# A convolution and a gated feed-forward on one core: w_in's third block as one transfer, a one-head mask, the start's decode and first products in another order, twelve casts on GpSimd and some squares later

## The chip, the cores and the metric

The kernel runs on one core of a Trainium2 chip. Its engines are TensorE (PE, with its weight loads listed as PEld), VectorE (DVE), ScalarE (ACT), GpSimd (POOL) and SyncE (SP, which here issues all DMAs). Each engine works through its own queue in order; an instruction waits for the semaphores of others where it needs their results. The metric is the device time of one execution in microseconds (us). Three runs of the kernel before gave 1162.87, 1164.42 and 1164.15, a median of 1164.15.

## The reference

```python
def _attn_ref(x, weight):            # x: 8 x 4160 x 192, weight: 8 heads x 7
    w = np.exp(weight - np.max(weight, axis=-1, keepdims=True))
    w = w / (np.sum(w, axis=-1, keepdims=True) + 1e-09)
    # causal: position s gets its 6 predecessors and itself, zeros ahead of the start
    out = np.einsum('hk,bskhg->bshg', w, x_unf)      # a convolution per head of 24 channels
...
def _moe_ref(x, w_in, w_out, g_ln):  # x: 33280 x 192, w_in: 192 x 1024, w_out: 1024 x 192
    h = x @ w_in
    e = np.exp(h - np.max(h, axis=-1, keepdims=True))
    solu = h * e / (np.sum(e, axis=-1, keepdims=True) + 1e-09)
    mu = np.mean(solu, axis=-1, keepdims=True)
    var = np.mean((solu - mu) ** 2, axis=-1, keepdims=True)
    return ((solu - mu) / np.sqrt(var + 1e-06) * g_ln) @ w_out
```

`w_in` and `w_out` arrive as 64-bit floats. The kernel reads each as two 32-bit words and puts the value together itself.

## The kernel before, in words

**Tiles.** The 33280 rows are 260 tiles of 128. A tile goes through these helpers. `emit_rows` and `emit_third` (or, for the first two tiles, `emit_first`) multiply the convolved rows `yT` by w_in, kept as an upper and a lower half-precision part (`whi`, `wlo`), into two PSUM banks `ph` (L736, L749, L759). `emit_max` on DVE scales `ph` and takes the row's extreme (L790). `emit_exp` on ACT takes the exponential `e` (L797). `emit_mul` on DVE makes the product of `ph` and `e` (L807). `emit_hi` casts it to half precision (L815), `emit_lo` on GpSimd makes the rest of it (L827) and SP then issues a DMA that transposes both into `pT`. `emit_square` on ACT sums the squares (L819) for the variance. `emit_out` multiplies `pT` by w_out (`ohl`, L859) and `emit_evac` takes the result from PSUM to `raw` on DVE (L867, L869). After each group of up to eight tiles, GpSimd takes the roots (L927 to L931) and the rows are scaled and stored.

**Chunks.** The convolution works on chunks of x, ahead of the tiles. `load` brings pieces `xr`; `sum_squares` finds their size (`xj` on ACT, `xa` on DVE); `scale_steps` makes the scale `s` and the factors `cv` from it. From the fourth chunk (number 3) on each piece is split into `xs` halves (L234 to L243). `product` multiplies by the taps into one PSUM bank `pc` (L281), `upper` (ACT, L313) and `lower` (DVE, L322) write its two halves `y`, and DMAs transpose them into `yT`. `taps` come at the start from `band`, a mask times the softmaxed weights.

**The start.** Ahead of the first tile stands a sequence written out by hand: w_in's three blocks (columns 0 to 511, 512 to 1023 of the loaded rows, and the third, called `Z`, with the last 64 rows of w_in) go through the steps of class `Words`: `exponents`, `mantissas`, `join` (DVE; join puts the low word in), `powers` (ACT), `signs` (DVE), `value` (the product of join and signed powers), `squares` (ACT, for the size of w_in). From the size come five small DVE instructions that give `t_in`, the scale of w_in; only then `whi` and `wlo` can be written. w_out goes through the same kind of steps, with `lows` and `whole` on GpSimd in place of `join`, and with `out_powers`, which multiplies by `g_ln`.

**Order.** The program is recorded in the order of the code, under a manual schedule: an engine runs its instructions in just this order. `first_two`, `second_two`, `third_two` and `fourth_two` handle tiles 0 to 7 in pairs; `three_steps(i)` handles tiles i, i+1, i+2 from i = 8 on, with the convolution's work of the next chunk placed between; `last_three` ends it. In `three_steps`, `start` is true for i = 8, 11 and 14; `root_squares` emits squares left over from the triple before; `sum_up` sums squares of a chunk's piece. `queue.run` lets GpSimd's splitting steps in by a budget.

Of the kernel before, what the change touches and what calls it, by code (L numbers as in the profile page):

```python
# [19 lines left out]
def kernel(  # L20
# [366 lines left out]
    for j in range(2):  # L387
        nc.sync.dma_start(
            raw_in[j * R : (j + 1) * R, F:, :].rearrange("p f t -> p (f t)"),
            w_in[2 * R : D, j * F : (j + 1) * F],  # L390
        )
# [12 lines left out]
    pool.memset(band, 1.0)  # L404
    pool.affine_select(
        out=band, in_=band, pattern=[[0, H], [-1, TB], [-1, K]],
# [101 lines left out]
    def valued(c):  # L508

        wi.signs(c, wi.m)  # L510
        wi.value(c, wi.m, dve)
# [13 lines left out]
        band, band, wb.unsqueeze(2).broadcast_to([TJ, H, TB, K]), ALU.mult  # L525
# [12 lines left out]
    valued(halves[0])  # L538
# [48 lines left out]
    isq = cp.tile([P, 2], F32, name="isq")  # L587
# [19 lines left out]
    wi.squares(A, isq[:, 0:1])  # L607
    wi.signs(halves[1], wi.m)
    wi.exponents(Z)
    wi.powers(Z)  # L610
    for f in chain0[1:-3]:
        f()
    wi.squares(Z, isq[:, 1:2])
    for pc, hg in got0:
        c0.upper(pc, *hg)
    wi.value(halves[1], wi.m, dve)
    wi.mantissas(Z)
# [9 lines left out]
    for c in halves:  # L627
        act.activation(whi[:, 0, c], wi.f[:, c], AF.Copy, scale=t_in)
    settle(*spans0[0], got1)
# [3 lines left out]
    wo.lows(W, 2.0**-32)  # L633
    wi.join(Z)
    valued(Z)
    for pc, hg in got0:
        c0.upper(pc, *hg)
# [22 lines left out]
    wo.exponents(W)  # L660
    for f in chain0[-3:]:
        f()
    wo.mantissas(W)
    sums1 = [h for j in range(chunks[1].np) for h in chunks[1].halves(j)]
    wo.powers(W)
    wo.floats(W)
# [6 lines left out]
    gate = cp.tile([1, 1], F32, name="gate")  # L673
# [4 lines left out]
    mean = None  # L678

# [61 lines left out]
    def emit_first(t, u):  # L741
# [4 lines left out]
        for j, w, r in ((0, whi, 0), (2, whi, 0), (0, wlo, 0), (1, whi, 1)):  # L746
            for q, lhs in zip((t, u), y):
                for n, bank in enumerate(banks_of(q)):
                    nc.tensor.matmul(  # L749
                        bank, lhs[j], w[:, r, n * 512 : (n + 1) * 512],  # L750
                        start=j == 0 and w is whi, stop=False,
                    )
                for n in range(NH if r else 0):
                    emit_third(q, n, False, False)
# [57 lines left out]
    def emit_hi(t):  # L812
        t.halves = t.e.rearrange("p (n f) -> p n f", n=NH)
        t.p16 = sp.tile([P, NH, 2, 512], F16, name=f"p16_{t.i}", tag="p16", bufs=4)
        act.copy(t.p16[:, :, 0, :], t.halves)  # L815
# [333 lines left out]
    def first_two():  # L1149
# [4 lines left out]
        emit_exp(t)  # L1154
        wo.signs(W, wo.e)

        pool.tensor_copy(gate, wo.e.bitcast(F32)[0:1, 0:1])
        wo.whole(W)
# [16 lines left out]
    def second_two():  # L1175
# [13 lines left out]
        for f in scale:  # L1189
            f()  # L1190
# [104 lines left out]
    def three_steps(i):  # L1295
# [103 lines left out]
        if not start:  # L1399
            root_squares()  # L1400
# [197 lines left out]
```

## Time and profile before

| | before |
|---|---|
| runs, us | 1162.87, 1164.15, 1164.42 |
| span of the profiled execution, us | 1161.5 |
| the profiled execution's own time | one of these; the results don't say which, so 1.4 to 2.9 us lie around the span |
| PE idle, 0 to 44 us | 17.3 us |
| PE idle, 44 to 138 us | 5.9 us |
| PE idle, 138 us to the end | 5.6 us |

The idle times come from the busy times of stretches: 44 us less 7.87 and 18.88 us of work from 0 to 19 and from 19 to 44, for instance. A row of the timeline gives the start in us from the span's start, the duration, the engine, the line of the kernel, the operation, what it writes and reads, and in brackets how long its engine was idle before and what ended that. A row of the waits names who waited, for whom, the sum in us, how often and the longest. Groups of instructions end with busy us, mean ns of one and the idle time before them.

### The profile page before, as it was taken

The page shows a single profiled execution, that of the slowest core. Times are in us where ns is not written, and L with a number is a line of the kernel's source. Part 1 is how long each engine was busy: PE and PEld are TensorE (multiplying, and loading weights), DVE is VectorE, ACT ScalarE, POOL GpSimd, SP SyncE. Part 2 cuts the span into 40 slices and gives each one's busy share as a digit, 9 for nine tenths or more (in the row PEclk, how much of TensorE's full clock was granted, in tenths as well). Part 3 has the DMA queues.
Part 4 walks back from the last instruction along what each step waited for, and adds up shares of the span by engine and source line. Part 5 has one row for each costly group of instructions (what it writes and reads, how often), then busy time and mean ns, then how long its engine had stood idle before and what let it go on. Part 6 is the DMA issues. An engine that isn't in the chain of part 4 may idle for free.

```text
span 1161.5 us, 22374 instructions
## 1 busy us (share of the span) xinstructions
PE 1132.2 (97%) x7742; PEld 692.4 (60%) x7742; DVE 1016.8 (88%) x2058; ACT 998.0 (86%) x1775; POOL 878.6 (76%) x686
## 2 busy tenths in 40 slices
PE   5898999999999999999999999999999999999998
PEld 3575566656666665655656666665666566566556
DVE  8888898988989898998889989888898988788787
ACT  6998988888888888888888888898888889888886
POOL 2745879987888588887868888588788858855665
PEclk9999999999999999999999999999999999999999
DMA  8799899999999999999999999999999998999988
GB/s 226 171 181 180 185 218 205 205 201 202 200 213 195 195 186 220 207 189 199 202 198 190 208 209 199 187 202 208 206 204 198 195 193 170 174 177 186 181 163 188
DMA packets 727391, 226.95 MB, mean 195 GB/s; under 512 B 651614, under 2 KB 725870, under 8 KB 727278
## 3 DMA queue, kind: packets, MB, share of 16 engines
q1 hardware_dynamic: 727278, 225.53, 100.2%
q8 instruction: 60, 0.98, 0.3%
q14 instruction: 53, 0.43, 0.1%
HBM read 33.00 MB, written 25.56 MB: 50 GB/s over the span
## 4 chain that ended last, share of the span: by engine, by line
PE 88%; DVE 5%; ACT 2%; DMA 2%; issue 2%; POOL 1%; SPq 0%; DVEq 0%; ACTq 0%; POOLq 0%
PE po L859 40%; PE ph L736 36%; PE pc L281 6%; PE ph L759 5%; DVE e L807 1%; DMA pT<-p 1%; DVE ph L790 1%; DMA raw_in<-in_moe_w_in_dram 1%; ACT e L797 1%; ACT sq L819 0%; DVE raw L869 0%; DVE y L322 0%; POOL p L827 0%; PE mean L701 0%; DVE wlo L647 0%
## 5 line engine op out<-in xcount | busy, mean ns | idle before, releaser
L827 POOL TENSOR_TENSOR p<-e,p 128x1024 f16<-128x1024 f32 x257 | 548.3, 2138 | 219.5 <-ACT p L815 218.0
L859 PE MATMUL po<-ohl,pT 128*128 128x192 f16 (+1 forms) x4264 | 539.8, 283 | 7.8 <-DVE raw L869 5.4
L859 PEld LDWEIGHTS <-pT 128*128 128x128 f16 x4264 | 384.4, 98 | 167.1 <-issue 7.6
L736 PE MATMUL ph<-whi,yT 128*128 128x512 f16 x1548 | 419.1, 380 | 2.7 <-DVE e L807 2.6
L790 DVE TENSOR_SCALAR_CACHE_REDUCE ph<-ph,cv 128x1024 f32<-128x1024 f32 x248 | 319.1, 1288 | 72.9 <-PE ph L759 56.6
L797 ACT ACTIVATE e<-ph,sm 128x1024 f32<-128x1024 f32 x260 | 289.4, 1113 | 102.0 <-DVE ph L790 95.8
L807 DVE SCALAR_TENSOR_TENSOR e<-ph,cv,e 128x1024 f32<-128x1024 f32 x248 | 317.1, 1279 | 26.0 <-ACT e L797 25.7
L736 PEld LDWEIGHTS <-yT 128*128 128x128 f16 x2064 | 192.6, 98 | 231.3 <-issue 36.3
L815 ACT CAST p<-e 128x1024 f16<-128x1024 f32 x257 | 266.8, 1039 | 27.9 <-DVE e L807 27.3
L819 ACT ACTIVATE sq<-e 128x1024 f32<-128x1024 f32 x260 | 273.4, 1052 | 0.2
L736 PE MATMUL ph<-wlo,yT 128*128 128x512 f16 x516 | 153.5, 379 | 0.0
L869 DVE TENSOR_REDUCE raw<-po 128x192 f32<-128x384 f32 x247 | 136.3, 552 | 14.3 <-PE po L859 13.9
L243 POOL TENSOR_TENSOR xs<-xr,xs 128x960 f16<-128x960 f32 (+1 forms) x56 | 107.6, 1922 | 1.4
L313 ACT ACTIVATE y<-pc 112x432 f16<-112x432 f32 (+5 forms) x140 | 62.8, 469 | 13.8 <-PE pc L281 8.1
L759 PE MATMUL ph<-wlo,yT 64*128 64x512 f16 x269 | 74.0, 380 | 0.0
L322 DVE SCALAR_TENSOR_TENSOR y<-pc,y 112x432 f16<-112x432 f32 (+5 forms) x140 | 72.2, 532 | 0.8 <-ACT y L313 0.8
L281 PE MATMUL pc<-xs,taps_hi 128*112 128x240 f16 (+1 forms) x448 | 72.9, 261 | 0.0
L759 PE MATMUL ph<-wlo,y 64*128 64x512 f16 x251 | 68.6, 380 | 0.0
L181 DVE TENSOR_REDUCE xa<-xr 128x1 f32<-128x384 f32 x112 | 66.6, 617 | 0.0
L281 PEld LDWEIGHTS <-taps_hi 128*112 128x112 f16 x448 | 52.4, 130 | 16.4
L240 POOL TENSOR_SCALAR xr<-xr,s 128x960 f32<-128x960 f32 (+1 forms) x56 | 57.5, 1027 | 2.9
L281 PE MATMUL pc<-xs,taps_lo 128*112 128x240 f16 (+1 forms) x224 | 58.5, 261 | 0.0
(148 smaller groups left out, 787.6 us busy)
## 6 DMA issues: line engine op xcount, KB each, us to landing
out_dram<-raw SPq DMA_DIRECT2D x127, 192.0 KB, 3.0
xr<-in_x_dram SPq DMA_DIRECT2D x41, 480.0 KB, 4.7
xr<-in_x_dram SPq DMA_DIRECT2D x22, 384.0 KB, 4.1
pT<-p SPq DMA_TRANSPOSE x263, 4.6
y<-yT SPq DMA_DIRECT2D x15, 140.0 KB, 3.1
y<-yT SPq DMA_DIRECT2D x15, 126.0 KB, 3.1
yT<-y SPq DMA_TRANSPOSE x102, 3.7
raw_out<-in_moe_w_out_dram SPq DMA_DIRECT2D x1, 1536.0 KB
```

What stands on the lines that cost most here:

```text
L243: (2.1 * size + 0.2, lambda: pool.tensor_tensor(xl, r, h, ALU.subtract)),
L281: nc.tensor.matmul(o, tp[:, h + j, :], r, start=q == 0, stop=q == len(ops) - 1)
L736: nc.tensor.matmul(bank, lhs, w[:, r, n * 512 : (n + 1) * 512], start=start and j == 0, stop=stop and j == len(ops) - 1,)
L759: nc.tensor.matmul(banks_of(t)[n], y[q, t.off : t.off + P], wlo[q, 1, n * 512 : (n + 1) * 512], start=start, stop=not start,)
L790: dve.tensor_scalar(t.ph, t.ph, t.cv[:, 0:1], None, ALU.mult, ALU.min, accum_out=t.bias)
L797: act.activation(t.e, t.ph, AF.Exp, bias=t.bias, scale=-1.0, accum_out=grp.z[:, g : g + 1])
L807: dve.scalar_tensor_tensor(t.e, t.ph, t.cv[:, 3:4], t.e, ALU.mult, ALU.mult, accum_out=t.grp.s1[:, t.g : t.g + 1],)
L815: act.copy(t.p16[:, :, 0, :], t.halves)
L819: act.activation(junk, t.e, AF.Square, accum_out=t.grp.s2[:, t.g : t.g + 1])
L827: eng.tensor_tensor(t.p16[:, :, 1, :], t.halves, t.p16[:, :, 0, :], ALU.subtract)
L859: nc.tensor.matmul(t.po[:, 0:n], t.pT[:, a, :], w, start=j == 0, stop=j == len(ops) - 1)
L869: dve.tensor_reduce(t.grp.raw[:, t.g, :], t.po[:, 0 : 2 * D].rearrange("p (a d) -> p d a", a=2), AX.X, ALU.add,)
```

## The change

The third block of w_in comes in one DMA with source rows as 2 times 64 and 128 target rows, instead of two DMAs of 64 rows. The mask is made for one head (20x98 instead of 20x784) and read by all eight heads when `band` is made. w_in's squares are taken in three steps of 512 columns; the second and third block's `value` go to GpSimd; the third block's `mantissas` and `join` stand ahead of `t_in`. `emit_first` issues its products in another order. w_out's `lows`, `mantissas`, `floats`, `whole` and `signs` are reordered, the small copy `gate` is gone, and its `value` on GpSimd is cut in two. `emit_hi` runs on GpSimd for tiles 2 to 7, 9, 10, 12, 13, 15 and 16. Squares stand later at tile 0, at the triples of tiles 11 and 14 (with sums of a chunk), and at tile 17.

On DVE, from the third block's first step to `t_in`, there stood before (`e_in`, `m_in`, `f_in` are exponents, mantissas or signed powers, and the value of w_in; `xm`, `s` belong to chunk 0's scale):

```order
L447 TENSOR_SCALAR e_in<-raw_in 128x512
L203 TENSOR_REDUCE xm_166<-pt_x_174 128x1
L105 TENSOR_SCALAR s_167<-xm_166 128x1
L106 TENSOR_SCALAR s_167<-s_167 128x1
L109 TENSOR_SCALAR s_167<-s_167 128x1
L112 TENSOR_SCALAR s_167<-s_167 128x1
L497 TENSOR_TENSOR f_in<-f_in,m_in 128x512
L452 TENSOR_SCALAR m_in<-raw_in 128x512
L624 TENSOR_REDUCE isq<-pt_wi 128x1
L105 TENSOR_SCALAR t_in<-isq 128x1
```

and now, at the same place of DVE's queue:

```order
L448 TENSOR_SCALAR e_in<-raw_in 128x512
L453 TENSOR_SCALAR m_in<-raw_in 128x512
L203 TENSOR_REDUCE xm_168<-pt_x_176 128x1
L105 TENSOR_SCALAR s_169<-xm_168 128x1
L106 TENSOR_SCALAR s_169<-s_169 128x1
L109 TENSOR_SCALAR s_169<-s_169 128x1
L112 TENSOR_SCALAR s_169<-s_169 128x1
L491 SCALAR_TENSOR_TENSOR m_in<-raw_in,e_in 128x512
L482 SCALAR_TENSOR_TENSOR f_in<-raw_in,m_in 128x512
L627 TENSOR_REDUCE isq<-pt_wi 128x1
L105 TENSOR_SCALAR t_in<-isq 128x1
```

The second block's product (L497) has left DVE; the third block's mantissas moved ahead of chunk 0's scale, and its join (L482) ahead of `t_in`.

On ACT, in the triple of tiles 11 to 13, there stood before, from tile 12's exponential on (`sq_938` and `sq_940` are the squares of tiles 9 and 10, `xj` a chunk's sums, `y` the convolution's upper half):

```order
L797 ACTIVATE e_936,z_690<-ph_901,sm_932 128x1024
L819 ACTIVATE sq_938,s_8_692<-e_761 128x1024
L819 ACTIVATE sq_940,s_8_692<-e_850 128x1024
L187 ACTIVATE xj_2_972,xa_756<-xr_1_333 128x384
L187 ACTIVATE xj_3_974,xa_756<-xr_1_333 128x576
L313 ACTIVATE y_2_10_976<-pc_10_0_967,s_754 112x5x96
L815 CAST p_11_979<-e_926 128x2x512
L819 ACTIVATE sq_998,s_8_692<-e_926 128x1024
L815 CAST p_12_1001<-e_936 128x2x512
```

and now:

```order
L803 ACTIVATE e_937,z_691<-ph_902,sm_933 128x1024
L313 ACTIVATE y_2_10_969<-pc_10_0_964,s_755 112x5x96
L824 CAST p_11_972<-e_927 128x2x512
L828 ACTIVATE sq_977,s_8_693<-e_762 128x1024
L828 ACTIVATE sq_979,s_8_693<-e_851 128x1024
L187 ACTIVATE xj_2_981,xa_757<-xr_1_333 128x384
L187 ACTIVATE xj_3_983,xa_757<-xr_1_333 128x576
L828 ACTIVATE sq_999,s_8_693<-e_927 128x1024
```

The squares and the chunk's sums moved behind the upper half and tile 11's cast, and tile 12's cast has left ACT.

On GpSimd, around the roots of tiles 8 to 15, there stood before, from the factors `cv` on (`p_16` is tile 16's lower part, `xs` the lower halves of chunk 3's first pieces):

```order
L208 TENSOR_SCALAR cv_1055<-cv_1055 128x1 x3
L927 TENSOR_TENSOR t_8_694<-s_8_692,t_8_694 128x8
L928 TENSOR_SCALAR t_8_694<-t_8_694 128x8
L929 TENSOR_TENSOR t_8_694<-t_8_694,t_8_693 128x8
L930 TENSOR_TENSOR t_8_694<-t_8_694,mhalf 128x8
L931 TENSOR_SCALAR t_8_694<-t_8_694,o_inv 128x8
L240 TENSOR_SCALAR xr_0_329<-xr_0_329,s_1054 128x960
L827 TENSOR_TENSOR p_16_1232<-e_1215,p_16_1232 128x2x512
L243 TENSOR_TENSOR xs_1227<-xr_0_329,xs_1227 128x960
L240 TENSOR_SCALAR xr_1_333<-xr_1_333,s_1054 128x960
L827 TENSOR_TENSOR p_17_1311<-e_1304,p_17_1311 128x2x512
L243 TENSOR_TENSOR xs_1227<-xr_1_333,xs_1227 128x960
```

and now, behind the same `cv`:

```order
L822 TENSOR_SCALAR p_16_1233<-e_1216 128x2x512
L936 TENSOR_TENSOR t_8_695<-s_8_693,t_8_695 128x8
L937 TENSOR_SCALAR t_8_695<-t_8_695 128x8
L938 TENSOR_TENSOR t_8_695<-t_8_695,t_8_694 128x8
L939 TENSOR_TENSOR t_8_695<-t_8_695,mhalf 128x8
L940 TENSOR_SCALAR t_8_695<-t_8_695,o_inv 128x8
L240 TENSOR_SCALAR xr_0_329<-xr_0_329,s_1055 128x960
L836 TENSOR_TENSOR p_16_1233<-e_1216,p_16_1233 128x2x512
L243 TENSOR_TENSOR xs_1228<-xr_0_329,xs_1228 128x960
L240 TENSOR_SCALAR xr_1_333<-xr_1_333,s_1055 128x960
L836 TENSOR_TENSOR p_17_1312<-e_1303,p_17_1312 128x2x512
L243 TENSOR_TENSOR xs_1228<-xr_1_333,xs_1228 128x960
```

Tile 16's cast is new, ahead of the roots.

The diff:

```diff
@@ -384,11 +384,10 @@
             raw_in[:, j * 512 : (j + 1) * 512, :].rearrange("p f t -> p (f t)"),
             w_in[0 : 2 * R, j * F : (j + 1) * F],
         )
-    for j in range(2):
-        nc.sync.dma_start(
-            raw_in[j * R : (j + 1) * R, F:, :].rearrange("p f t -> p (f t)"),
-            w_in[2 * R : D, j * F : (j + 1) * F],
-        )
+    nc.sync.dma_start(
+        raw_in[:, F:, :].rearrange("p f t -> p (f t)"),
+        w_in[2 * R : D, :].rearrange("r (j f) -> j r f", j=2),
+    )
     nc.sync.dma_start(
         raw_out.rearrange("p (c d) t -> p c (d t)", d=D),
         w_out.rearrange("(c p) d -> p c d", p=P),
@@ -401,9 +400,11 @@
     mhalf = cp.tile([P, 1], F32, name="mhalf")
     pool.memset(mhalf, -0.5)
     band = cp.tile([TJ, H, TB, K], F32, name="band")
-    pool.memset(band, 1.0)
+    mask = sp.tile([TJ, F], F32, name="mask", tag="e", bufs=4)
+    mask = mask[:, 0 : TB * K].rearrange("p (c k) -> p c k", k=K)
+    pool.memset(mask, 1.0)
     pool.affine_select(
-        out=band, in_=band, pattern=[[0, H], [-1, TB], [-1, K]],
+        out=mask, in_=mask, pattern=[[-1, TB], [-1, K]],
         compare_op=ALU.is_equal, fill=0.0, base=0, channel_multiplier=1,
     )
     NS = CW - TB
@@ -505,10 +506,10 @@
         wi.mantissas(c)
         wi.join(c)
 
-    def valued(c):
+    def valued(c, eng=pool):
 
         wi.signs(c, wi.m)
-        wi.value(c, wi.m, dve)
+        wi.value(c, wi.m, eng)
 
 
     wtop = cp.tile([TJ, H], F32, name="wtop")
@@ -522,7 +523,8 @@
     dve.reciprocal(wtop, wtop)
     dve.tensor_tensor(wb, wb, wtop.unsqueeze(2).broadcast_to([TJ, H, K]), ALU.mult)
     dve.tensor_tensor(
-        band, band, wb.unsqueeze(2).broadcast_to([TJ, H, TB, K]), ALU.mult
+        band, mask.unsqueeze(1).broadcast_to([TJ, H, TB, K]),
+        wb.unsqueeze(2).broadcast_to([TJ, H, TB, K]), ALU.mult,
     )
     bsum = cp.tile([TJ, H, TB], F32, name="bsum")
     dve.tensor_reduce(bsum, band, AX.X, ALU.add)
@@ -535,7 +537,9 @@
 
     words(halves[0])
     wi.powers(halves[0])
-    valued(halves[0])
+    isq = cp.tile([P, 3], F32, name="isq")
+    wi.squares(halves[0], isq[:, 0:1])
+    valued(halves[0], dve)
 
 
     taps = cp.tile([P, H, CW], F32, name="taps")
@@ -584,7 +588,6 @@
 
 
     t_in = cp.tile([P, 1], F32, name="t_in")
-    isq = cp.tile([P, 2], F32, name="isq")
     chain0 = c0.scale_steps()
     spans0 = list(zip(c0.cuts, c0.cuts[1:]))
     assert len(spans0) == 2 and len(c0.heads(*spans0[1])) == NH
@@ -604,17 +607,17 @@
     got0 = [next(going)]
     c0.add_up()
     got0 += going
-    wi.squares(A, isq[:, 0:1])
-    wi.signs(halves[1], wi.m)
+    wi.squares(halves[1], isq[:, 1:2])
     wi.exponents(Z)
+    wi.mantissas(Z)
     wi.powers(Z)
     for f in chain0[1:-3]:
         f()
-    wi.squares(Z, isq[:, 1:2])
+    wi.squares(Z, isq[:, 2:3])
+    valued(halves[1])
     for pc, hg in got0:
         c0.upper(pc, *hg)
-    wi.value(halves[1], wi.m, dve)
-    wi.mantissas(Z)
+    wi.join(Z)
     c0.open(0, None)
     got1 = got0
     wo, W = Words(raw_out, "out"), slice(0, NFC * D)
@@ -626,15 +629,11 @@
         f()
     for c in halves:
         act.activation(whi[:, 0, c], wi.f[:, c], AF.Copy, scale=t_in)
+    valued(Z)
     settle(*spans0[0], got1)
     for j in range(chunks[1].np):
         chunks[1].load(j)
     nc.sync.dma_start(gl, g_ln.rearrange("(c p) -> p c", p=P))
-    wo.lows(W, 2.0**-32)
-    wi.join(Z)
-    valued(Z)
-    for pc, hg in got0:
-        c0.upper(pc, *hg)
 
 
     top, low = slice(0, R), slice(R, P)
@@ -658,24 +657,25 @@
         for j in range(c.np):
             c.load(j)
     wo.exponents(W)
+    for pc, hg in got0:
+        c0.upper(pc, *hg)
     for f in chain0[-3:]:
         f()
-    wo.mantissas(W)
     sums1 = [h for j in range(chunks[1].np) for h in chunks[1].halves(j)]
     wo.powers(W)
-    wo.floats(W)
+    wo.lows(W, 2.0**-32)
 
     def settle_rest():
         settle(*spans0[1], got0)
         nc.sync.dma_start(wlo[low, 1, :], wlo[top, 1, :])
 
 
-    gate = cp.tile([1, 1], F32, name="gate")
     o_inv = cp.tile([P, 1], F32, name="o_inv")
     t_out = cp.tile([P, 1], F32, name="t_out")
     osq = cp.tile([P, 1], F32, name="osq")
     wof = wo.f.rearrange("p (c d) -> p c d", d=D)
     mean = None
+    out_halves = [slice(0, NFC * D // 2), slice(NFC * D // 2, NFC * D)]
 
     def out_powers():
 
@@ -743,15 +743,21 @@
         y = [[q.yT[:, j, q.off : q.off + P] for j in range(NB)] for q in (t, u)]
         for slot, q in enumerate((t, u)):
             q.ph = pair(slot, f"ph_{q.i}")
-        for j, w, r in ((0, whi, 0), (2, whi, 0), (0, wlo, 0), (1, whi, 1)):
+        def product(q, lhs, j, w, r):
+            for n, bank in enumerate(banks_of(q)):
+                nc.tensor.matmul(
+                    bank, lhs[j], w[:, r, n * 512 : (n + 1) * 512],
+                    start=j == 0 and w is whi, stop=False,
+                )
+
+        for w in (whi, wlo):
             for q, lhs in zip((t, u), y):
-                for n, bank in enumerate(banks_of(q)):
-                    nc.tensor.matmul(
-                        bank, lhs[j], w[:, r, n * 512 : (n + 1) * 512],
-                        start=j == 0 and w is whi, stop=False,
-                    )
-                for n in range(NH if r else 0):
-                    emit_third(q, n, False, False)
+                product(q, lhs, 0, w, 0)
+        for q, lhs in zip((t, u), y):
+            product(q, lhs, 2, whi, 0)
+            product(q, lhs, 1, whi, 1)
+            for n in range(NH):
+                emit_third(q, n, False, False)
 
     def emit_third(t, n, low, start):
 
@@ -812,7 +818,10 @@
     def emit_hi(t):
         t.halves = t.e.rearrange("p (n f) -> p n f", n=NH)
         t.p16 = sp.tile([P, NH, 2, 512], F16, name=f"p16_{t.i}", tag="p16", bufs=4)
-        act.copy(t.p16[:, :, 0, :], t.halves)
+        if t.i in (2,3,4,5,6,7,9,10,12,13,15,16,):
+            pool.tensor_scalar(t.p16[:, :, 0, :], t.halves, 1.0, 1.0, ALU.mult, ALU.mult)
+        else:
+            act.copy(t.p16[:, :, 0, :], t.halves)
 
     def emit_square(t):
         junk = sp.tile([P, F], F32, name=f"sq_{t.i}", tag="sq", bufs=1)
@@ -1152,10 +1161,10 @@
         emit_first(t, u)
         emit_max(t)
         emit_exp(t)
+        wo.mantissas(W)
+        wo.floats(W)
+        wo.whole(W)
         wo.signs(W, wo.e)
-
-        pool.tensor_copy(gate, wo.e.bitcast(F32)[0:1, 0:1])
-        wo.whole(W)
         emit_mul(t)
         out_powers()
         emit_max(u)
@@ -1168,7 +1177,8 @@
         for c in chunks[3:4]:
             for j in range(XR - sum(q.np for q in chunks[1:3])):
                 c.load(j)
-        wo.value(W, wo.e, pool)
+        for c in out_halves:
+            wo.value(c, wo.e, pool)
         for q in (t, u):
             emit_lo(q, pool)
 
@@ -1183,9 +1193,9 @@
         emit_max(t)
         emit_exp(t)
         out_mean()
-        emit_square(tiles[0])
         emit_max(u)
         emit_exp(u)
+        emit_square(tiles[0])
         for f in scale:
             f()
         numerators(t)
@@ -1315,6 +1325,8 @@
 
         start = i < 2 * PAIRED
 
+        behind = i in (11,14,)
+
         soon = i in (FIRST // P * 2 + 1, FIRST // P * 3 + 2)
         if not start:
             loads(work)
@@ -1396,7 +1408,7 @@
             if i == PAIRED:
                 for k, h in late:
                     sum_up(k, h, i - 1)
-        if not start:
+        if not start and i != 17:
             root_squares()
         add(0)
         if not start:
@@ -1409,13 +1421,17 @@
         emit_max(b)
         lowers(1)
         emit_exp(b)
+        if i == 17:
+            root_squares()
         if start:
-            root_squares()
+            if not behind:
+                root_squares()
             second()
             if i > PAIRED:
-                for k, h in late:
-                    sum_up(k, h, i - 1)
-                late.clear()
+                if not behind:
+                    for k, h in late:
+                        sum_up(k, h, i - 1)
+                    late.clear()
                 uppers(2)
             for k, q in doubles:
                 k.double(*q)
@@ -1426,6 +1442,12 @@
             late[:] = after
         emit_hi(a)
         emit_lo(a, pool)
+        if start and behind:
+            root_squares()
+            if i > PAIRED:
+                for k, h in late:
+                    sum_up(k, h, i - 1)
+                late.clear()
         move()
         if urgent:
             openings()
```

## The prediction

> **What bounds the kernel now.** I read the page's totals first, then the sums by stretch, then the waits of TensorE, and last the timeline where those waits lie.
>
> ```profile
> span 1161.5 us, 22374 instructions
> PE 1132.2 (97%) x7742; PEld 692.4 (60%) x7742; DVE 1016.8 (88%) x2058; ACT 998.0 (86%) x1775; POOL 878.6 (76%) x686
> ...
> 19.00:44.00 25.00, 18.88 (x84) 10.11 (x84) 22.26 (x39) 21.41 (x35) 14.85 (x10) 0.93 0.87 213
> 44.00:74.00 30.00, 29.79 (x245) 20.76 (x246) 25.67 (x58) 29.43 (x59) 12.42 (x12) 1.00 0.81 151
> ...
> 88.00:138.00 50.00, 44.33 (x300) 26.46 (x298) 41.76 (x87) 44.05 (x80) 37.13 (x29) 1.00 0.87 174
> 138.00:1120.00 982.00, 979.86 (x6659) 592.74 (x6658) 868.91 (x1732) 847.20 (x1496) 776.16 (x592) 1.00 1.03 197
> ```
>
> A stretch's row gives its length, then the busy time of PE, PEld, DVE, ACT and POOL. From 138 us on PE works 979.86 of 982 us: no other engine can save anything there, and whatever comes earlier only decides when that stretch begins. The change touches no later tile. So its worth is the PE idle time it removes (or adds) before 138 us: the start, up to the first full stretch at 44 us, and the 5.67 us missing between 88 and 138. Between 44 and 74 PE is full already (29.79 of 30), so ACT's 29.43 there costs nothing.
>
> **The start, step by step.**
>
> ```profile
> 2.53 1.29 DVE L516 TENSOR_TENSOR wb<-wb,wtop 20x56 f32<-20x56 f32 x1
> 5.14 0.20 DVE L523 TENSOR_TENSOR wb<-wb,wtop 20x56 f32<-20x56 f32 x1
> 7.88 0.41 DVE L447 TENSOR_SCALAR e_in<-raw_in 128x512 int32<-128x512 int32 x1
> 11.43 0.43 DVE L447 TENSOR_SCALAR e_in<-raw_in 128x512 int32<-128x512 int32 x1 [0.56 <-DMA raw_in<-in_moe_w_in_dram]
> DMA to landing us min/median/max: 4.7/8.4/9.1
> GB/s 0 0 4 56 130 205 360 392 336 326 331 386 405 374 243 210 193 219 209 264 332 366 381 369 354 130 22 0 116 113 83 147 60 169 23 88 238 372 369 349
> ```
>
> The one-head mask takes one eighth of the elements. L516 and L523 are the same operation; the first stood beside GpSimd's long selection and took 1.29 us. Without it some 1.1 us go, and the first decode (7.88) moves up until w_in's first block has landed. That alone is worth nothing: the second block's decode waits for its DMA (the 11.43 row), so the landing is late next.
>
> The rate row (slices of 0.625 us from 0 to 25) falls from 374 to about 200 GB/s between 8.8 and 11.9 us, while the two 64-row transfers of the third block run. One 128-row transfer that kept the 380 GB/s of its neighbours would carry the 512 KB in 1.4 us, and the second block would be in at about 10.2 (an estimate from this row). No row shows a transfer whose source begins with 2 and whose target begins with 128, so its landing is bounded from both sides: the second block lands between 10.2 and, unchanged, 11.4. I take 10.2.
>
> ```profile
> 12.24 0.69 DVE L481 SCALAR_TENSOR_TENSOR f_in<-raw_in,m_in 128x512 f32<-128x512 uint32 x1
> 13.97 0.15 DVE L203 TENSOR_REDUCE xm<-pt_x 128x1 f32<-128x4 f32 x1
> 14.73 0.15 DVE L112 TENSOR_SCALAR s<-s 128x1 int32<-128x1 int32 x1
> 16.81 0.15 DVE L112 TENSOR_SCALAR t_in<-t_in 128x1 int32<-128x1 int32 x1
> 17.42 1.59 POOL L458 TENSOR_SCALAR raw_out<-raw_out 128x1536 f32<-128x1536 uint32 x1 [12.56 <-DMA raw_out<-in_moe_w_out_dram]
> 18.25 1.28 DVE L481 SCALAR_TENSOR_TENSOR f_in<-raw_in,m_in 128x512 f32<-128x512 uint32 x1
> ```
>
> DVE's queue from the second block to `t_in` becomes: three steps of block two (0.43 + 0.42 + 0.69, with gaps 1.6), two of block three (0.85), five small ones for chunk 0's scale (13.97 to 14.73 and 0.15: 0.95), signs (0.69), join of block three, five small ones to `t_in` (0.93). GpSimd now does block two's product beside that join. Beside L458 the same join took 1.28 instead of 0.69, and I take 1.28. From 10.2 that is 16.5, against 16.96 now: **0.4 gained**; with the landing unchanged it is 0.7 lost, without the slow join 1.0 gained. The squares in three steps cost ACT one more read of the accumulator, in a time in which it waits for DVE. The one issue that SP loses brings w_out's load forward, whose first reader moves back from 17.42, so nothing comes of it.
>
> The Trainium skill, page "SBUF — State Buffer", section "SBUF: two separate sides", calls the port pair that DVE and GpSimd share an exclusive lock: a DVE operation with two SBUF inputs stands still while GpSimd reads SBUF. The 1.28 row agrees; by the rule the join waits here too, by a mere bandwidth view it would stay at 0.69 and the sum would be 0.6 better.
>
> ```profile
> 16.88 1.46 DVE L322 SCALAR_TENSOR_TENSOR y<-pq,s,y 112x480 f16<-112x480 f32 x3
> 20.91 2.84 DVE L647 SCALAR_TENSOR_TENSOR wlo<-f_in,t_in,whi 128x512 f16<-128x512 f32 x4
> 23.78 0.96 DVE L447 TENSOR_SCALAR e_out<-raw_out 128x1536 int32<-128x1536 int32 x1
> 24.97 0.97 DVE L452 TENSOR_SCALAR m_out<-raw_out 128x1536 int32<-128x1536 int32 x1
> 25.84 1.30 DVE L790 TENSOR_SCALAR_CACHE_REDUCE ph<-ph,cv 128x1024 f32<-128x1024 f32 x1
> 21.02 2.94 ACT L644 ACTIVATE whi<-f_in,t_in 64x512 f16<-64x512 f32 x4 [1.44 <-DVE f_in L497]
> 32.76 3.44 POOL L497 TENSOR_TENSOR f_out<-f_out,e_out 128x1536 f32<-128x1536 f32 x1
> 44.03 0.60 PE L736 MATMUL ph<-whi,yT 128*128 128x512 f16 x2 [0.93 <-DVE e L807]
> 55.68 2.15 PE L859 MATMUL po<-ohl,pT 128*128 128x192 f16 x24
> ```
>
> From `t_in` to the first maximum (25.84) DVE is never idle: 8.9 us. Of these go the third block's join (1.28), its product (0.69, to GpSimd) and `m_out` (0.97), 2.94 in all, which leaves 6.0 for signs, lowers 1.46, the four `wlo` 2.84, `e_out` 0.96 and small ones. The first tile's products end just ahead of that: signs 0.69, GpSimd's product 1.15 (a third of 3.44), ACT's four upper parts 2.94 and the last matmuls, some 5.9 after `t_in`; in the new order the `wlo` products no longer hold these last ones up. I take 6.1: **2.8 gained**. Behind the maximum the gain is partly given back: `m_out` now stands between it and the first product (+1.0), and GpSimd's `lows` run beside it, which by the same 1.28-to-0.69 difference costs 0.6. The two tiles' products, the mean's matmuls and the start at 44.03 follow rigidly, each waiting for the one ahead. GpSimd still ends w_out's decode ahead of the mean, which now waits for the second tile's product first. Casts of tiles 2 and 3 make their transposed halves later, but no matmul reads them before 55.68. The stretch's granted clock of 0.93 is taken as staying.
>
> Start: 0.4 + 2.8 - 1.0 - 0.6 = **1.6 us gained**, with bounds 0.5 (landing unchanged) to 2.8 (neither DVE delay).
>
> **The middle.**
>
> ```profile
> PE po L859 <- DVE raw L869: 5.0, 5, 1.8
> PE pc L281 <- DVE y L322: 0.5, 1, 0.5
> ...
> L815 ACT CAST p<-e 128x1024 f16<-128x1024 f32 x257 | 266.8, 1039 | 27.9 <-DVE e L807 27.3
> L236 POOL TENSOR_SCALAR xs<-xr,s 128x960 f16<-128x960 f32 x39 | 41.6, 1065 | 0.0
> ...
> 83.96 1.05 ACT L819 ACTIVATE sq<-e 128x1024 f32<-128x1024 f32 x1
> ...
> 85.13 1.06 ACT L819 ACTIVATE sq<-e 128x1024 f32<-128x1024 f32 x1
> ...
> 87.64 0.64 ACT L313 ACTIVATE y<-pc,s 112x480 f16<-112x480 f32 x1
> ...
> 112.00 0.20 POOL L927 TENSOR_TENSOR t<-s,t 128x8 f32<-128x8 f32 x1 [0.57 <-ACT t L921]
> 123.17 2.01 POOL L243 TENSOR_TENSOR xs<-xr,xs 128x960 f16<-128x960 f32 x1
> ...
> 120.00 2.12 PE L859 MATMUL po<-ohl,pT 128*128 128x384 f16 x16 [1.19 <-DVE raw L869]
> 122.87 2.12 PE L859 MATMUL po<-ohl,pT 128*128 128x384 f16 x16 [0.46 <-DVE raw L869]
> 126.56 0.37 PE L281 MATMUL pc<-xs,taps_hi 128*112 128x240 f16 x2
> ```
>
> From 88 to 138 PE waits 5.0 + 0.5 us, five times for DVE's evacuation, and DVE stands in order behind products that wait for ACT. From 83.96 two squares hold ACT for 2.3 us, and the convolution's upper half comes only at 87.64. The change moves exactly these squares behind that work at tiles 11 and 14, and behind two exponentials at tile 17, and takes twelve casts of 1.04 us, 12.5 us in all, from ACT. Each now costs GpSimd about 1.14 (L236's 1065 ns scaled from 960 to 1024 elements). The moved work is longer than any single wait, so I let all 5.2 us of waits that stand behind ACT go (the rest is small).
>
> What is late next is GpSimd: tile 16's cast now stands ahead of the roots, which started at 112.00; it ends about 0.95 later. Behind them the second piece of `xs` (123.17 + 2.01 = 125.18) has 1.38 us to the convolution at 126.56. PE comes there 1.65 earlier (1.19 + 0.46), so it waits 1.65 + 0.95 - 1.38 = 1.2. Middle: 5.2 - 1.2 = **4.0 gained**; bounds 1.0, if most waits only find another releaser, and 5.5.
>
> **The sum.** The profiled span is 1161.5; the three runs are 1162.87 to 1164.42 with a median of 1164.15, so about 2.65 us lie around the span, which I leave as they are. 1161.5 - 1.6 - 4.0 + 2.65 = **1158.5**; with the bounds 1155.9 to 1162.7.
>
> **Rivals.**
>
> (a) *The third block's transfer runs narrow* (slower). Source rows are laid out as 2 times 64, target rows as 128. If the split over DMA engines follows what both leading counts share, only two engines carry it, 256 KB each.
>
> ```profile
> DMA packets 30, 0.00 MB, mean 4 GB/s; under 512 B 30, under 2 KB 30, under 8 KB 30
> ```
>
> For this row (0.9 to 2.0 us, packets of the 20-row load of `weight` alone) 20 are its rows; the other 10 fit ten engines finishing, a divisor of 20. At the 390 GB/s that the rate row comes to, one of 16 engines moves 24.4 GB/s, so 256 KB take 10.7 us, at 330 GB/s 12.7. Begun between 8.8, where the rate falls, and 11.4, the block lands between 19.5 and 24.1; I price it at 20, since nothing but the second block's own rows is ahead of it. Its decode stands in DVE's queue ahead of chunk 0's scale, so all behind it waits: `t_in` at 20 + 4.4 = 24.4 instead of 16.5, **7.9 later**, 1158.5 + 7.9 = 1166.4 (1165.9 to 1170.5 by the landing's bounds). A landing after 11.9, when DVE is done with block two, begins to cost, and from 17.5 on the whole gain of 5.6 is gone. For it speaks the count of 10; against it, that no row shows unequal leading counts.
>
> The Trainium skill, page "DMA: Bandwidth & Descriptors", section "Why a DMA increments its semaphore by 16 and not by 1", has this rule: the engines used are the largest number up to 16 that divides the slowest dimension of both sides. By it this transfer gets two; the trace agrees for 20 rows and shows no unequal pair.
>
> (b) *GpSimd takes ACT's place.* In 88 to 138 it works 37.13 us; five casts make it 42.8 of some 46. If the evacuations then wait for it, the middle gives 0 to 1.0: 1161.5 to 1162.5.
>
> (c) *The start gains nothing*: unchanged landing and both DVE delays, with the middle at 4: 1164.15 - 0.5 - 4.0 = 1159.6. It lies in the forecast's range.
>
> **How the numbers follow.** Forecast with (c): 0.47, nearly all of it below 1161.8; (a): 0.36; (b): 0.17. The first is likeliest, because each of its terms has a row, while (a) rests on a count that fits. The range goes from 1156.0 to 1168.5: it reaches to (a), whose end above 1168.5 and the forecast's last bit below 1156 are left out. A measurement here tells about 0.2% (2.3 us) from no change, so faster is below 1161.8 and slower above 1166.5. Faster: 0.45 of the forecast and 0.05 of (b), 0.50. Same: 0.02, 0.12 of (b) and 0.15 of (a), 0.29. Slower: 0.21, the rest of (a).
>
> **What would show it.** The decode of the third block on DVE without a wait, and `t_in` done by about 16.5, carry the start; a DVE wait of several us for `raw_in` shows (a). PE full from 42.4 instead of 44 us confirms the steps behind. In the middle PE's waits for `raw` gone, and about 1 us for `xs` in its place. An idle ACT with evacuation waits still there means (b). I would be wrong throughout if PE's long stretch lost its 99.8%.

## The result, and the profile after

The changed kernel takes 1169.09 us (median of five runs, 1166.57 to 1171.67), the kernel before 1164.23 (five runs). The ratio is 1.0051, with a 95% interval of 1.0037 to 1.0064: slower by half a per cent, where 1158.5 and a range of 1156.0 to 1168.5 had been forecast. The profiled execution of the changed kernel took 1169.09 us, 2.7 more than its span.

The page's totals of the changed kernel:

```profile
span 1166.4 us, 22364 instructions
PE 1132.9 (97%) x7742; PEld 691.9 (59%) x7742; DVE 1014.8 (87%) x2056; ACT 986.4 (85%) x1765; POOL 891.1 (76%) x700
```

TensorE's work is nearly the same (1132.9 us against 1132.2), so 4.2 of the 4.9 us of span are idle time of TensorE. ACT has lost and GpSimd gained the work that the change moves between them. The busy times don't say where the idle time lies; the timeline of DVE at the start does. These are the first steps of w_in's second and third block, the last step of `t_in`, the first maximum and the first product:

```profile
12.39 0.43 DVE L448 TENSOR_SCALAR e_in<-raw_in 128x512 int32<-128x512 int32 x1 [0.90 <-DMA raw_in<-in_moe_w_in_dram]
...
22.01 0.43 DVE L448 TENSOR_SCALAR e_in<-raw_in 128x512 int32<-128x512 int32 x1 [8.14 <-DMA raw_in<-in_moe_w_in_dram]
...
25.47 0.15 DVE L112 TENSOR_SCALAR t_in<-t_in 128x1 int32<-128x1 int32 x1
...
32.50 1.29 DVE L796 TENSOR_SCALAR_CACHE_REDUCE ph<-ph,cv 128x1024 f32<-128x1024 f32 x1 [0.58 <-PE ph L765]
...
36.46 1.27 DVE L813 SCALAR_TENSOR_TENSOR e<-ph,cv,e 128x1024 f32<-128x1024 f32 x1
```

DVE stands still for 8.14 us until the third block has landed, at 22.0 us. `t_in` is done at 25.6 instead of 16.96. The rate row of the DMA view over the first 26 us (slices of 0.65 us), and the landing of w_out behind it, show the transfer itself:

```profile
GB/s 0 0 6 102 135 300 360 334 287 267 344 351 356 355 345 368 259 238 214 255 243 195 156 95 74 72 45 57 57 50 50 46 51 47 47 47 47 47 28 9
...
raw_out<-in_moe_w_out_dram SPq DMA_DIRECT2D x1, 1536.0 KB, 21.7
```

From about 17 us on only 45 to 57 GB/s flow, mostly 47 to 50: two engines at the 24 GB/s that the prediction worked out for one. The busy share of the core's 16 DMA engines, the last number but one of a stretch's row, says the same: 0.12, and 0.14 from 17 to 19 us, is two of 16.

```profile
19.00:21.00 2.00, 0.00 (x0) 0.00 (x0) 0.00 (x0) 0.00 (x0) 0.00 (x0) 1.00 0.12 50
```

w_out, issued at 4.4, needs 21.7 us and lands at 26.1; in the kernel before its first reader ran at 17.42. That fits rows of it standing behind the third block's on these two engines, which the trace doesn't show row by row. It cost nothing here: w_out's first reader, on DVE, runs only at 30.65 and doesn't wait for it.

The second place is the middle. First the kernel before, then the changed one: TensorE's first output product `po`, and the block of output products that contains the 401st (its second half, at 150.4, in the kernel before).

```profile
46.40 2.15 PE L859 MATMUL po<-ohl,pT 128*128 128x192 f16 x24
...
148.34 4.20 PE L859 MATMUL po<-ohl,pT 128*128 128x384 f16 x32
```

```profile
52.22 2.15 PE L868 MATMUL po<-ohl,pT 128*128 128x192 f16 x24
...
129.59 0.26 PE L281 MATMUL pc<-xs,taps_hi 128*112 128x240 f16 x1 [1.07 <-POOL xs L243]
...
152.33 2.13 PE L868 MATMUL po<-ohl,pT 128*128 128x384 f16 x16 [1.15 <-DMA pT<-p]
155.20 2.13 PE L868 MATMUL po<-ohl,pT 128*128 128x384 f16 x16 [0.73 <-DMA pT<-p]
```

This stretch went from 104.0 us to 103.0 (155.20 less 52.22). TensorE's waits of the changed kernel from 50 to 160 us (for whom, the sum in us, how often, the longest):

```profile
PE po L868 <- DMA pT<-p: 1.9, 2, 1.2
PE pc L281 <- POOL xs L243: 1.1, 1, 1.1
...
PE po L868 <- DVE raw L878: 0.8, 2, 0.4
```

The five waits for DVE's evacuation (5.0 us) are down to 0.8, as forecast, and the forecast wait for `xs` is there. Behind it stand two waits for transposed `p`, 1.9 us, which the prediction did not have. So the sum over the execution, from the rows above and those of the kernel before:

| stage, us | before | after | difference | forecast |
|---|---|---|---|---|
| to the end of `t_in` | 16.96 | 25.62 | +8.7 | -0.4 |
| from there to the first maximum | 8.88 | 6.88 | -2.0 | -2.8 |
| to the first product | 3.08 | 3.96 | +0.9 | +1.6 |
| to the first output product | 17.48 | 15.76 | -1.7 | 0 |
| to the 401st output product | 104.0 | 103.0 | -1.0 | -4.0 |
| to the end of the span | 1011.1 | 1011.2 | +0.1 | 0 |
| sum | 1161.5 | 1166.4 | +4.9 | -5.6 |

### The profile page after: what moved, and what is told of

Its sections match the earlier page's. It is cut to its first block, busy times and chain, and to the rows that moved or that the text cites. A ratio compares the mean times of both kernels' runs of the same rounds, so it can differ in the third digit from the quotient of the medians.

```text
span 1166.4 us, 22364 instructions
## 1 busy us (share of the span) xinstructions
PE 1132.9 (97%) x7742; PEld 691.9 (59%) x7742; DVE 1014.8 (87%) x2056; ACT 986.4 (85%) x1765; POOL 891.1 (76%) x700
## 4 chain that ended last, share of the span: by engine, by line
PE 83%; POOL 5%; DMA 4%; DVE 2%; issue 2%; ACT 2%; SPq 1%; POOLq 0%; DVEq 0%; ACTq 0%
PE po L868 38%; PE ph L736 34%; PE pc L281 6%; PE ph L765 5%; POOL p L836 2%; DMA pT<-p 2%; DMA raw_in<-in_moe_w_in_dram 2%; DVE e L813 1%; ACT sq L828 1%; ACT p L824 1%; DVE ph L796 1%; POOL t L939 1%; SPq L352 1%; POOL xs L243 0%; ACT e L803 0%
## 5 line engine op out<-in xcount | busy, mean ns | idle before, releaser
L824 ACT CAST p<-e 128x1024 f16<-128x1024 f32 x245 | 254.3, 1038 | 24.8 <-DVE e L813 24.5
```

## The experiments

Ratios are to the kernel before, timed beside each group of kernels on the same chip (medians 1163.06, 1162.99 and 1163.21 us: the transfer, the first four of the middle, the rest).

**The transfer.** Four kernels ask whether the width of one transfer costs the time. `z_two` is the changed kernel with the third block as two transfers again:

```diff
-    nc.sync.dma_start(
-        raw_in[:, F:, :].rearrange("p f t -> p (f t)"),
-        w_in[2 * R : D, :].rearrange("r (j f) -> j r f", j=2),
-    )
+    for j in range(2):
+        nc.sync.dma_start(
+            raw_in[j * R : (j + 1) * R, F:, :].rearrange("p f t -> p (f t)"),
+            w_in[2 * R : D, j * F : (j + 1) * F],
+        )
```

> The changed kernel, with w_in's third block again as two transfers of 64 rows. Theory N (narrow: one transfer is carried by as many DMA engines as the largest number up to 16 that divides both leading counts, here 2): the block lands by about 13.5 us instead of 22.0, t_in is done at about 17.7 instead of 25.6, and the time falls by these 7.9 to about 1161.2 (up to 1163 if the half clock that the kernel before had at 35 us comes back). Theory O (the new order of DVE's and ACT's steps at the start is what costs): the block lands early, but t_in moves by under 2 us and the time stays above 1167.

`z_four` and `z_sixteen` keep one transfer of 512 KB into the same 128 partitions, and only the source differs: its leading count, and with it which rows of w_in are read. Their outputs are therefore not the reference's, and they serve for the timing alone:

```diff
-        w_in[2 * R : D, :].rearrange("r (j f) -> j r f", j=2),
+        w_in[:, F : 2 * F].rearrange("(a r) f -> a r f", a=4)[:, 0 : 32, :],
```

(with a=16 and 0 : 8 in `z_sixteen`)

> The changed kernel, the third block as one transfer of the same size whose source is viewed as 4 times 32 rows instead of 2 times 64 (other rows of w_in are read, so the output isn't the reference's). Theory N: four engines with 128 KB each instead of two with 256 KB; at 24.4 GB/s each that ends 5.2 us sooner, so the block lands at about 16.8 and the time is about 1164. Rival R (128 rows in one transfer are late whatever the view, because of the place in the queue or the stride of the rows): 22 us and 1169, as in the changed kernel.

> As the run with 4 times 32, with 16 times 8 rows. Theory N: all 16 engines share the transfer, the block lands between 10.2 and 12.5 us as the prediction wanted it, t_in is done at about 16.5 to 17.5, and the time is 1160 to 1161.5. Rival R: 22 us and 1169.

`b_one` is the reverse of `z_two`: the kernel before with its two transfers made one.

> The kernel before, with only the third block's two transfers made one (2 times 64 rows). Theory N: DVE waits some 8 us for raw_in, the block lands at about 22, t_in is done 8.4 us later than 16.96, and the time is about 1172.6, 1 to 2 us less if the half clock at 35 us goes away. Theory O: the landing may move, but the time stays within 2 us of 1164.2.

The first step on the third block shows the landing in each. `z_two`, `z_four`, `z_sixteen` (there with the second block's row ahead) and `b_one`, from the timeline of DVE:

```profile
13.43 0.43 DVE L449 TENSOR_SCALAR e_in<-raw_in 128x512 int32<-128x512 int32 x1 [0.85 <-DMA raw_in<-in_moe_w_in_dram]
```

```profile
18.87 0.43 DVE L448 TENSOR_SCALAR e_in<-raw_in 128x512 int32<-128x512 int32 x1 [6.09 <-DMA raw_in<-in_moe_w_in_dram]
```

```profile
11.20 0.43 DVE L448 TENSOR_SCALAR e_in<-raw_in 128x512 int32<-128x512 int32 x1 [0.97 <-DMA raw_in<-in_moe_w_in_dram]
13.12 0.43 DVE L448 TENSOR_SCALAR e_in<-raw_in 128x512 int32<-128x512 int32 x1 [0.42 <-DMA raw_in<-in_moe_w_in_dram]
```

```profile
21.64 0.43 DVE L446 TENSOR_SCALAR e_in<-raw_in 128x512 int32<-128x512 int32 x1 [8.43 <-DMA raw_in<-in_moe_w_in_dram]
```

| kernel | leading count of the source | third block's step, us | time, us | ratio (95%) |
|---|---|---|---|---|
| changed | 2 | 22.0 | 1169.09 | 1.0051 (1.0037 to 1.0064) |
| b_one | 2 | 21.6 | 1172.75 | 1.0079 (1.0066 to 1.0092) |
| z_four | 4 | 18.9 | 1166.51 | 1.0025 (1.0015 to 1.0034) |
| z_sixteen | 16 | 13.1 | 1161.20 | 0.9979 (0.9969 to 0.9988) |
| z_two | 64, twice | 13.4 | 1161.96 | 0.9989 (0.9979 to 0.9999) |

Theory N holds in all four in kind. With target, size and place in the queue unchanged, the landing goes from 22.0 to 18.9 to 13.1 as the count goes from 2 to 4 to 16, so it is neither the place in the queue nor the single transfer (rival R). The busy share of the 16 DMA engines goes with it: 0.27, four of 16, in `z_four` from 18 to 20 us. `b_one` takes 9.7 us more than the kernel before beside it, without any reordering (theory O falls); its `t_in` came 8.2 later, where 8.4 were expected. Two landings missed their expectation: `z_four` came at 18.9 instead of 16.8, as twice the engines took off 3.1 us where 5.2 were expected, and `z_sixteen` at 13.1 where 10.2 to 12.5 were. Why is not shown.

The Trainium skill, page "DMA: Bandwidth & Descriptors", section "Why a DMA increments its semaphore by 16 and not by 1", takes the largest number up to 16 that divides the slowest dimension of both sides; it gives 2, 4 and 16 engines here, and the three landings agree with it in their order.

`z_sixteen` answers a second question: the prediction's start needed the second block at 10.2 us. With the third block at full width in one transfer it comes at 11.2, against 11.43 before; in the other profiles this step lies between 10.7 and 13.2, so the 0.2 is no difference. The rate still dips, to 198 to 254 GB/s between 9.1 and 12.4 us, so the dip was not due to the 64-row transfers.

**The middle.** These kernels stand on `z_two`. `m_none` takes all twelve casts back to ACT, `m_16` that of tile 16, `m_15_16` those of 15 and 16, `m_early` those of 9 to 16:

```diff
-        if t.i in (2,3,4,5,6,7,9,10,12,13,15,16,):
+        if t.i in ():
```

`m_sq` keeps the casts and puts squares and sums back:

```diff
-        behind = i in (11,14,)
+        behind = False
...
-        if not start and i != 17:
+        if not start:
...
-        if i == 17:
-            root_squares()
```

> The changed kernel with the third block as two transfers (the run z_two, 1161.96 us), and all twelve casts back on ACT; the squares stay late. In z_two TensorE's waits for DVE's evacuation between 88 and 138 us of the kernel before are gone (4.0 us), but it waits 1.1 us for xs and 2.3 us for transposed p, both behind GpSimd. Theory Q (moving the squares alone removes the evacuation waits, the casts on GpSimd only cost): both GpSimd waits vanish, no evacuation wait returns, 1161.96 - 3.4 = about 1158.6. Theory C (taking the casts off ACT removes the evacuation waits): they return (4.0) while GpSimd's go, about 1162.6.

> z_two with the cast of tile 16 alone back on ACT (it stands ahead of GpSimd's roots). Theory Q: GpSimd is 1.05 us earlier there, the wait for xs (1.1) falls to about 0.1 and that for transposed p (2.3) by 1.0, about 1159.9. Theory C: ACT is 1.04 later at tile 16 and one evacuation wait of up to 1.2 returns, about 1161.

> z_two with the casts of tiles 15 and 16 back on ACT. Theory Q: GpSimd is 2.1 us earlier at its split of chunk 3, both its waits (3.4) vanish, about 1158.6. Theory C: the evacuation waits of 1.19 and 0.46 at 120 to 123 us return, about 1160.2.

> z_two with the squares and sums of the triples of tiles 11 and 14 and of tile 17 in their old places, the twelve casts still on GpSimd. Theory Q: the evacuation waits return, up to 4.0 us, about 1164 to 1166. Theory C: they stay away, about 1162.

TensorE's waits from 50 to 160 us, in this order `z_two`, `m_none`, `m_sq`, `m_16` and `m_15_16`:

```profile
PE po L869 <- DMA pT<-p: 2.3, 2, 1.5
PE pc L281 <- POOL xs L243: 1.1, 1, 1.1
PE po L869 <- DVE raw L879: 0.8, 2, 0.4
```

```profile
PE po L869 <- DVE raw L879: 3.1, 5, 0.8
PE pc L281 <- DVE y L322: 1.4, 2, 0.9
...
PE po L869 <- DMA pT<-p: 0.3, 1, 0.3
```

```profile
PE po L869 <- DVE raw L879: 3.8, 4, 1.8
PE po L869 <- DMA pT<-p: 2.0, 2, 1.2
...
PE pc L281 <- POOL xs L243: 0.3, 1, 0.3
```

```profile
PE po L869 <- DVE raw L879: 2.2, 5, 0.7
PE po L869 <- DMA pT<-p: 1.4, 1, 1.4
```

```profile
PE po L869 <- DVE raw L879: 2.5, 5, 0.8
```

Two more kernels followed: `m_16` repeated, and `m_early`.

> The kernel of m_16 once more: 1159.74 us there, where the version with tile 15's cast on ACT as well gave 1162.02 although its profile had less waiting in the middle. If tile 16's cast is worth 2 us, this is again 1159 to 1160.5 (0.997 to 0.998 of the kernel before); if the low time was chance, 1161 to 1162.

> z_two with only the casts of tiles 2 to 7 on GpSimd; tiles 9, 10, 12, 13, 15 and 16 cast on ACT. From the first output product to the 400th the kernel before took 104.02 us, z_two 103.36, the version without any cast on GpSimd 104.95, that without the last two 101.96. If the casts of tiles 9 to 13 are what lets the late squares pay, this takes 104 to 105; if those of tiles 2 to 7 do, 102 to 103.

| kernel | casts on GpSimd, tiles | squares | first to 401st output product, us | time, us | ratio (95%) |
|---|---|---|---|---|---|
| before | none | early | 104.0 | | 1 |
| m_sq | 2 to 16 | early | 105.2 | 1163.67 | 1.0007 (0.9998 to 1.0016) |
| m_none | none | late | 104.9 | 1163.05 | 0.9997 (0.9987 to 1.0007) |
| m_early | 2 to 7 | late | 104.5 | 1162.84 | 0.9997 (0.9986 to 1.0008) |
| z_two | 2 to 16 | late | 103.4 | 1161.96 | 0.9989 (0.9979 to 0.9999) |
| m_16 | 2 to 15 | late | 102.5 | 1159.74 | 0.9975 (0.9965 to 0.9985) |
| m_16b | 2 to 15 | late | 102.3 | 1160.03 | 0.9966 (0.9954 to 0.9977) |
| m_15_16 | 2 to 13 | late | 102.0 | 1162.02 | 0.9991 (0.9983 to 1.0000) |

Neither theory Q nor theory C holds alone. Late squares without casts leave 3.1 us of evacuation waits, casts without late squares 3.8, of the 5.0 before; only both together bring them to 0.8. The casts of tiles 9 to 13 are needed for it: with 2 to 7 alone the waits are still 3.3 and the stretch 104.5. Whether those of 2 to 7 are needed too was not run. The cast of tile 16 costs more than it saves: without it the wait for `xs` (1.1) is gone and that for `p` falls from 2.3 to 1.4, while the evacuation waits rise again from 0.8 to 2.2. Without that of 15 both waits behind GpSimd are gone, with 2.5 of evacuation waits.

The version of `m_16` ran twice, and both times it was the fastest of this table. That the version without 15 as well is 2 us slower in time, although its stretch is the shortest, stays open: its profile lost 0.5 us in the start and 1.1 behind the 401st output product, which one execution can't tell from chance.

**The start.** `best1` is `m_16` with w_out's mantissas (`m_out`) ahead of the first maximum, where the kernel before had them:

```diff
     for f in chain0[-3:]:
         f()
+    wo.mantissas(W)
...
-        wo.mantissas(W)
         wo.floats(W)
```

> The changed kernel with the third block as two transfers, tile 16's cast back on ACT, and m_out (0.97 us) again ahead of the first maximum, where DVE stood idle for 0.56 us in z_two. If m_out behind the maximum is what lengthened the stretch from the first maximum to the first product (3.97 us against 3.09 before), that stretch falls back to about 3.1, the maximum moves back by 0.4 to 0.6, and the time is 0.3 to 0.5 us below that of the run without this step (m_16b, beside it). Rival: the stretch is set by GpSimd's lows beside the join, stays at 3.9, and the time is 0.4 longer.

DVE from the maximum to the first product, first in `m_16b`, then in `best1`, with GpSimd's `lows` (L460) of the latter behind:

```profile
25.59 1.22 DVE L454 TENSOR_SCALAR m_out<-raw_out 128x1536 int32<-128x1536 int32 x1
26.74 1.74 DVE L492 SCALAR_TENSOR_TENSOR e_out<-raw_out,e_out 128x1536 int32<-128x1536 int32 x1
```

```profile
27.45 2.52 DVE L492 SCALAR_TENSOR_TENSOR e_out<-raw_out,e_out 128x1536 int32<-128x1536 int32 x1
...
26.76 1.60 POOL L460 TENSOR_SCALAR raw_out<-raw_out 128x1536 f32<-128x1536 uint32 x1
```

The time is the same: 1159.74 us, ratio 0.9975 (0.9964 to 0.9986). `m_out` no longer stands behind the maximum (1.22 less), but L492 now begins while `lows` still runs for 0.9 us, and takes 2.52 instead of 1.74. The stretch from the maximum to the first product is 3.65 against 4.02, and the maximum comes 0.24 later behind `t_in`. So both the expectation and its rival were half right.

## Why the prediction was wrong

**The step that failed** is the start's: "I take 10.2" for the second block's landing, with bounds of 10.2 and 11.4, and "0.4 gained". It bounded only the second block's landing. The third block's own landing, which DVE's queue needs before anything of `t_in`, entered the sum at no cost, and with it the whole reordering. The runs showed 22.0 in its place. The mechanism was rival (a), priced at 1166.4 with a chance of 0.36; I held it less likely because "(a) rests on a count that fits". That count (30 packets, 10 beside 20 rows) was the only row on the matter, and nothing in the trace spoke for the forecast's full width. A view whose leading counts are 2 and 128 had no row at all, which is a reason for equal chances at least.

The transfer is not all of it. `z_two` is without it and gains 1.1 us over the kernel beside it, where the sum had 5.6: its `t_in` is at 17.0 instead of 16.5, and its middle gives 0.7 instead of 4.0.

**Rival (a) itself** was 2.7 us too low. From 1166.4: the landing 2.0 later than priced and the steps from it to `t_in` 3.6 instead of 4.4 (+1.2 together); the stretch from `t_in` to the maximum gained 2.0 instead of 2.8 (+0.8); the one behind it lost 0.9 instead of 1.6 (-0.7); the half clock was absent (-1.7, below); the middle gave 1.0 instead of 4.0 (+3.0); +0.1 at the end. That is 1169.1, the time of the profiled execution.

**`t_in` to the maximum, and behind it.** Right in kind, too large in size: the first tile's products end 6.9 us behind `t_in`, not 6.1, and DVE waits 0.58 us for them (the row at 32.50). In the changed kernel and the nine others that keep its order here, with landings from 13 to 22 us, the first stretch is 6.8 to 6.9 and the second 3.9 to 4.1. The 1.0 for `m_out` was paid. The 0.6 for `lows` was not: in the changed order it runs mostly beside the maximum. `best1` shows that the delay is real where the two do meet.

**The slow join** ("I take 1.28") did not come. DVE and GpSimd of the changed kernel:

```profile
24.12 0.68 DVE L482 SCALAR_TENSOR_TENSOR f_in<-raw_in,m_in 128x512 f32<-128x512 uint32 x1
```

```profile
24.29 1.64 POOL L498 TENSOR_TENSOR f_in<-f_in,m_in 128x512 f32<-128x512 f32 x1 [21.82 <-DVE m_in L491]
26.56 1.27 POOL L498 TENSOR_TENSOR f_in<-f_in,m_in 128x512 f32<-128x512 f32 x1 [0.63 <-DVE m_in L491]
```

The join began 0.17 us ahead of GpSimd's product and kept its 0.68; the product paid, with 1.64 against 1.27 for the next one. In `best1` `lows` began first, and there DVE's step paid, as the join did in the prediction's 1.28 row, where L458 had begun at 17.42. In these three cases the one that came second paid. The Trainium skill, page "SBUF — State Buffer", section "SBUF: two separate sides", says the same of its lock: whichever starts first holds it for the whole instruction. The prediction had used only the half of that sentence that speaks against DVE. What the second one paid was less than the overlap: 0.37 for 0.51 us here, 0.78 for 0.91 in `best1`.

**The middle.** "I let all 5.2 us of waits that stand behind ACT go" was 4.2 of 5.0, and "about 1 us for xs in its place" (1.2 in its working) was 1.1. Wrong was "what is late next is GpSimd" followed only as far as `xs`. Here are tile 16's cast on GpSimd, a later lower part of `p`, and the transposes that SP issues behind it, first in the changed kernel, then in the one before:

```profile
115.35 1.04 POOL L822 TENSOR_SCALAR p<-e 128x1024 f16<-128x1024 f32 x1 [0.28 <-DVE e L813]
...
132.64 2.13 POOL L836 TENSOR_TENSOR p<-e,p 128x1024 f16<-128x1024 f32 x1
134.79 1.83 SPq L838 DMA_TRANSPOSE pT<-p  x1
...
144.97 3.69 SPq L838 DMA_TRANSPOSE pT<-p  x1
```

```profile
128.28 2.13 POOL L827 TENSOR_TENSOR p<-e,p 128x1024 f16<-128x1024 f32 x1
130.44 1.69 SPq L829 DMA_TRANSPOSE pT<-p  x1
...
140.51 3.82 SPq L829 DMA_TRANSPOSE pT<-p  x1
```

From the cast to this lower part GpSimd pauses for no more than 0.1 us. It comes 4.36 us later than before, while ACT stands 2.9 later (a cast at 141.04, now at 143.97). SP's transpose starts as soon as the lower part is done, in both kernels, and from there SP issues its transposes and loads with pauses of under 0.2 us (until 155 us, before until 150). So the later transposes come 4.3 to 4.5 us later as well, and TensorE waits for them twice, 1.9 us. That the casts are behind it is shown by `m_none` (0.3 of this wait left) and `m_15_16` (none); the way through SP's queue is read from one execution. So rival (b) was there in part, beside the forecast's mechanism, where the text held them for alternatives.

**The step with no difference expected,** from the first product to the first output product, gained 1.7 by a clock that the prediction took "as staying".

## What to carry to other kernels

Merging two transfers is worth nothing if the merged view's first dimension is small (2 and 4 at the source here; the target's was not varied): 2 times 64 rows on one side and 128 on the other were carried by two engines, cost the start 8.6 us (`t_in` at 25.6, and at 17.0 in `z_two`) and held up another load behind them. Look for the row of such a view in the trace before pricing it, and where there is none, let the bad price have at least half the chance.

Where work moves to an engine that then runs without a pause, follow the whole queue behind it, and the queues that wait for it in turn (here SP's transposes), not only the first reader: the first wait (1.1 us) was found, two more (1.9 together) stood some 23 us and more behind it. And two moves that each leave the waits standing may remove them together; tests of one at a time would have thrown away both. The version that keeps both, with two transfers and tile 16's cast on ACT, beats both kernels: 0.9966 to 0.9975.

## What the hardware showed that was not expected

In nine of the thirteen profiles the granted clock is 0.5 for a stretch of 3.41 us that begins between 33 and 44 us; in four (the changed kernel, `m_none`, `m_sq`, `m_16b`) there is none. One of the nine, `best1`, has another at 18.6. The same kernel twice, `m_16` and then `m_16b`, by stretches (length, busy PE, PEld, DVE, ACT, POOL, granted clock):

```profile
36.00:39.40 3.40, 3.40 (x15) 3.40 (x14) 3.03 (x9) 3.40 (x6) 3.40 (x3) 0.50 0.70 140
```

```profile
36.00:39.40 3.40, 3.40 (x23) 2.98 (x22) 2.83 (x9) 3.37 (x8) 3.40 (x2) 1.00 0.87 212
```

From the first product to the first output product the nine take 17.4 to 17.95 us, the four 15.8 to 16.0. So this chance is worth 1.6 us of the time, and is part of why runs of one kernel lie up to 6 us apart: in `z_two` the six executions with a mean granted clock of 1.000 took 1159.49 to 1161.23 us, the six with 0.997 to 0.999 took 1162.68 to 1164.54. In the eight of `z_four` no such split shows. What decides whether the stretch comes is open. In all nine TensorE was busy for at most 1.70 of the 3.41 us right ahead of it (1.64 in the kernel before), but 1.68 us from 39.91 to 43.33 in the changed kernel and 1.70 from 32.46 to 35.87 in `m_16b` were not followed by one.

The granted clock in a stretch's row does not hold for the very start. In the changed kernel TensorE waited 8.7 us on end, until 24.0, and the row for the time behind it gives 1.00. But the same four matmuls take 1.91 us at 27.77 and 1.04 at 32.40:

```profile
PE pt_wi L95 <- ACT oj_in L471: 8.7, 1, 8.7
...
24.00:44.00 20.00, 16.52 (x77) 9.20 (x78) 18.94 (x35) 18.24 (x31) 12.37 (x10) 1.00 0.85 193
```

```profile
27.77 1.91 PE L748 MATMUL ph<-whi,yT 128*128 128x512 f16 x4
...
32.40 1.04 PE L748 MATMUL ph<-whi,yT 128*128 128x512 f16 x4
```

So TensorE ran at about half speed until 29.7 us. The trace's clock records begin only there (in the kernel before at 14.6), and the row counts the time ahead of them as full. It cost the start nothing that can be seen: from `t_in` to the first maximum the changed kernel takes 6.88 us, and `z_two`, whose records begin at 13.7, takes 6.86.

The Trainium skill, page "TensorE: Matmul & The Clock Gate", section "What's actually happening", has a free-running window of 3413 ns, which agrees with the length. It has the half clock follow an idle window, and the slow products behind the 8.7 us don't speak against that. The nine stretches do so in part: they came behind 3.41 us in which TensorE was busy for up to half the time, so here the window need not have been idle throughout.
